# Taking out twenty waits between VectorE and GpSimd in a gated convolution and spectral-filter kernel

## The chip, the cores and the metric

The kernel runs on one core of one Trainium2 chip. The metric is the device time of one execution in microseconds (us). The engines are named as in the profile: PE (TensorE, matrix products into PSUM), DVE (VectorE), ACT (ScalarE), POOL (GpSimd, which works on SBUF alone and issues DMAs of its own), SP (SyncE, which here only issues DMAs).

## The reference, cut to what matters

Input q, k, v and x have 2048 positions and 640 channels. A first branch convolves k with a causal kernel of four taps per channel, multiplies by v, convolves the result with a causal kernel of 2048 taps per channel (by FFT) and multiplies by q. A second branch multiplies the two-dimensional spectrum of q by a complex weight. A gate, one number per position, mixes the two.

```python
def reference(A_q, A_k, A_v, A_shift_k, A_ssm_k, A_ssm_D, B_x, B_w_r, B_w_i, gate_w):
    x = A_q
    g = sigmoid((x * gate_w).sum(-1, keepdims=True))
    # a: k_shift = causal 4-tap convolution of k; kv = k_shift * v
    #    y = causal convolution of kv with ssm_k over 2048 positions + kv * ssm_D;  a = q * y
    # b: irfft2(rfft2(x) * (w_r + 1j * w_i))
    return g * a + (1 - g) * b
```

## The kernel before

All Fourier transforms are done as matrix products with constant matrices on PE, in stages of 32 and 64 points, with 32 by 32 block transposes on DVE between them. The work is cut into units, each with a name and a number, and each unit into operations numbered from 0:

- `fwd` u (u = 0 to 7): loads an eighth of q transposed (`xT`), folds it by four operations on SBUF, two adding and subtracting at L301 from XX into M, two at L303 from M back into XX, then multiplies on PE (L309, L316) and lets ACT copy the result into XX.
- `b1`, `bs2`, `i1`, `u`, `dic`: the second branch, the stages of the spectrum of q. In `bs2` the weight w multiplies the spectrum (L389, L392) and two operations at L395 combine the parts into XX. In `dic` ACT scales the result, two operations at L465 and two at L467 unfold it in M, and a DMA takes it to the output, added to what is there (POOL, L471) or plainly (SP, L474).
- `kv` u, `h` u (0 to 9): the first branch's data. `kv` loads k and v, makes the four-tap convolution on PE (L486), multiplies by v (DVE, L489), folds it in two operations at L495 and transposes (DVE, L498). `h` loads the long kernel, lets ACT negate one half (L507), adds another piece to it with an accumulating DMA that POOL issues (L508), and adds the ssm_D term in one short DVE operation (L511).
- `s1Y`, `s1H`, `s2`, `is1`, `afin`: transforms of kv and h on PE with DVE transposes into YY (L530, L540), their product in `s2` (PE L560, ACT L565, multiplications at L578 and L581, sums at L586), the inverse transform (PE L271, DVE L276), and in `afin` the product with q and the output.

The elementwise operations on SBUF are made by a helper `ttop` (L217). Each can run on POOL or on DVE; a set written out by hand, `ON_DVE` (L23), tells which run on DVE. The order in which everything is issued is written out as well, in `ORDER` (L40): each engine, and each of the two DMA queues that SP and POOL feed, works through its own part of that list in order. Semaphores between the engines follow from the tiles that operations read and write.

Every operation carries a pair `port` (L175, L220). The first number is 1 for what `ttop` made. The second is 1 where the operation, run on DVE, has both of its operands in SBUF; an operation of `ttop` that on DVE reads PSUM instead (those with `alt`, at L389, L578 and L628) has 0. `gate_cols` (L290) and the short operation of `h` (L512) are marked by hand. Beside the semaphores of the data, `_emit` (L702) adds a further wait when `GATE` (L34) is true: after each DVE operation marked with the second number, the next POOL operation in the list that is marked with the first waits for it, whether or not it has to do with its data. One wait stands for all DVE operations marked before it, and POOL operations behind it in the queue come later by themselves. DVE never waits for POOL on this ground.

Twenty pairs result. In the order of the list, unit number and operation number of POOL's operation behind those of DVE's:

| POOL waits at | for DVE's | POOL waits at | for DVE's |
|---|---|---|---|
| fwd 2 (4), L303 | fwd 2 (3), L303 | bs2 5 (4), L389 | bs2 0 (10), L395 |
| fwd 4 (2), L301 | kv 0 (5), L495 | bs2 3 (9), L395 | kv 6 (4), L495 |
| fwd 6 (2), L301 | fwd 6 (1), L301 | kv 9 (4), L495 | h 9, L511 |
| fwd 6 (4), L303 | kv 1 (5), L495 | s2 15 (11), L586 | s2 15 (10), L586 |
| fwd 7 (3), L303 | h 1, L511 | dic 1 (7), L465 | dic 1 (6), L465 |
| fwd 5 (2), L301 | fwd 5 (1), L301 | dic 4 (6), L465 | h 8, L511 |
| kv 4 (5), L495 | fwd 3 (4), L303 | kv 8 (4), L495 | dic 2 (7), L465 |
| kv 5 (4), L495 | h 3, L511 | dic 5 (8), L467 | dic 5 (7), L465 |
| s2 5 (4), L578 | s2 4 (10), L586 | dic 3 (9), L467 | dic 3 (8), L467 |
| s2 6 (10), L586 | h 4, L511 | dic 7 (9), L467 | dic 7 (8), L467 |

At dic 5 the operation waited for is also one whose result POOL's operation reads.

Of the kernel before, what the change touches and what calls it, by code (L numbers as in the profile page):

```python
# [30 lines left out]
    "afin": [(0, 4), (2, 4), (3, 4), (4, 4), (5, 4), (6, 4), (7, 4), (7, 6), (8, 4), (9, 4), (9, 6)],  # L31
    "dic": [(0, 9), (1, 6), (2, 6), (2, 7), (2, 8), (2, 9), (3, 7), (3, 8), (4, 8), (4, 9), (5, 6), (5, 7), (7, 6), (7, 7), (7, 8)],
}.items() for i, k in l}
GATE = True  # L34
HRAW = set()
FIRST=(3,3)
BACK={7,9}
# [664 lines left out]
def _emit(tc, plan):  # L702
# [4 lines left out]
    with tc.manual_schedule():  # L707
        for i in ORDER:
            o = plan.ops[i]
            made = o.fn()  # L710
            if GATE and o.eng == "DVE" and o.port[1]:
                ahead = made
# [70 lines left out]
```

## Time and profile before

| | us |
|---|---|
| three runs | 283.7, 286.7, 291.62 |
| their median | 286.7 |
| the profiled execution: time | 283.68 |
| its span, from first to last instruction | 281.6 |
| busy: PE, DVE, POOL, ACT | 246.3, 224.1, 150.1, 103.6 |

The profile is of one execution. Times in its rows count from the start of the span. In a row of the timeline stand the start, the length, the engine, the line of the kernel, the operation, what it writes and reads with the shapes, how many instructions the row holds, and in brackets the idle time of the engine before it and what ended that. In the chain of waits, each piece is what the next one waited for, up to the instruction that ended last; "issue" is time in which an engine waited for nothing that the profile can name, and a DMA counts from its issue to its landing. A transfer or an operation is named by the tile it writes and the tile it reads (XX<-xT). An operation that stands at its engine without getting its data shows as a longer one, not as idle time.

### The profile page before, as it was taken

Reading aid. Unit: us, or ns where it says so; the run is one execution under the profiler, and the core shown is the slowest. Engines: PE = TensorE matmul, PEld = TensorE weight load, DVE = VectorE, ACT = ScalarE, POOL = GpSimd, SP = SyncE. Lnnn points to the kernel's source line nnn. Section 1 sums busy time; section 2 is a strip of 40 time slices with the busy share of each in tenths; the row PEclk is TensorE's granted clock in tenths of the full one; section 3 lists DMA queues with packets and bytes.
Section 4 is the critical chain, followed back from the end, with each engine's and each line's share of the span. In section 5 each row is a group of like instructions: output and inputs, shape, how many; then the busy total and the mean of one; then the engine's idle time right before and its main releaser. Section 6 shows DMA issues by size and latency. Waiting matters only on the chain.

```text
span 281.6 us, 10200 instructions
## 1 busy us (share of the span) xinstructions
PE 246.3 (87%) x4562; PEld 144.9 (51%) x4562; DVE 224.1 (80%) x250; ACT 103.6 (37%) x232; POOL 150.1 (53%) x116
## 2 busy tenths in 40 slices
PE   0798789899999999788998988999999999999950
PEld 0674445554334454125445433667776677776450
DVE  3979489759998999999999999896464895664970
ACT  1052404451233333362263030546644374445500
POOL 0047557535005574798989710079888328339420
PEclk9999979999999999999999999999999999999996
DMA  7999979959996255687269963626548538737789
GB/s 277 421 416 346 330 264 420 410 123 365 278 389 230 70 98 199 188 338 254 82 165 352 260 121 99 276 80 231 146 115 139 131 54 149 228 54 97 134 200 211
DMA packets 28251, 61.53 MB, mean 218 GB/s; under 512 B 1712, under 2 KB 18480, under 8 KB 26544
## 3 DMA queue, kind: packets, MB, share of 16 engines
q1 hardware_dynamic: 22512, 51.45, 49.8%
q0 software_dynamic: 5696, 9.44, 21.9%
q8 instruction: 36, 0.59, 0.8%
q14 instruction: 7, 0.06, 0.1%
HBM read 50.39 MB, written 10.49 MB: 216 GB/s over the span
## 4 chain that ended last, share of the span: by engine, by line
PE 64%; DVE 15%; DMA 8%; POOL 5%; issue 4%; SPq 1%; ACT 1%; DVEq 0%; POOLq 0%; ACTq 0%
PE banks L560 11%; PE banks L271 11%; PE banks L356 7%; PE banks L447 7%; PE banks L420 7%; PE banks L530 5%; PE banks L622 5%; DMA XX<-xT 4%; DMA V<-h 4%; DVE YY L540 3%; DVE XX L276 3%; PE banks L309 3%; PE banks L453 2%; PE banks L486 2%; PE banks L428 2%
## 5 line engine op out<-in xcount | busy, mean ns | idle before, releaser
L540 DVE STREAM_TRANSPOSE YY<-banks 128x1024 f32<-128x1024 f32 x40 | 48.2, 1227 | 8.4 <-PE banks L530 8.4
L560 PE MATMUL banks<-YY,s2a 64*32 64x256 f32 x1280 | 43.0, 389 | 2.7 <-issue 1.6
L565 ACT ACTIVATE H<-banks 128x512 f32<-128x512 f32 x40 | 23.5, 598 | 39.9 <-PE banks L560 20.2
L495 POOL TENSOR_TENSOR T<-V 128x512 f32<-128x512 f32 x12 | 15.8, 1330 | 41.8 <-DVE V L489 22.0
L560 PEld LDWEIGHTS banks<-YY,s2a 64*32 64x32 f32 x1280 | 24.0, 105 | 19.7 <-issue 6.7
L271 PE MATMUL banks<-YY,ca 32*64 32x512 f32 x512 | 31.1, 607 | 0.6 <-DVE YY L540 0.4
L309 PE MATMUL banks<-cc,XX 128*64 128x162 f32 (+1 forms) x256 | 22.1, 330 | 8.7 <-DVE cc L287 8.7
L612 ACT ACTIVATE V<-V,g 128x128 f32<-128x128 f32 x72 | 21.9, 394 | 14.4 <-DMA V<-q 14.4
L309 PEld LDWEIGHTS banks<-cc,XX 128*64 128x64 f32 x256 | 19.4, 150 | 14.2 <-DVE cc L287 8.7
L581 DVE TENSOR_TENSOR YY<-banks,H 128x512 f32<-128x512 f32 x24 | 16.3, 682 | 13.1 <-ACT H L565 12.8
L276 DVE STREAM_TRANSPOSE YY<-banks 128x2048 f32<-128x2048 f32 x10 | 23.1, 2313 | 3.3 <-PE banks L271 2.9
L303 POOL TENSOR_TENSOR XX<-M 128x640 f32<-128x640 f32 x8 | 12.4, 1557 | 19.3 <-DVE XX L303 13.7
L461 ACT ACTIVATE M<-banks,om 128x320 f32<-128x320 f32 x32 | 14.2, 528 | 21.9 <-PE banks L453 16.2
L395 POOL TENSOR_TENSOR XX<-M,M 128x642 f32<-128x642 f32 x15 | 19.7, 1328 | 4.1 <-DVE M L389 3.4
L271 PEld LDWEIGHTS banks<-YY,ca 32*64 32x64 f32 x512 | 13.3, 129 | 15.5 <-issue 10.6
L356 PE MATMUL banks<-XX,cb 128*128 128x512 f32 (+1 forms) x42 | 20.9, 632 | 0.0
L622 PEld LDWEIGHTS banks<-YY,is2a 128*64 128x64 f32 x320 | 18.1, 134 | 5.3 <-DVE YY L540 1.9
L622 PE MATMUL banks<-YY,is2a 128*64 128x128 f32 x320 | 20.3, 279 | 0.5 <-DVE YY L276 0.5
L447 PEld LDWEIGHTS banks<-di,L 128*128 128x128 f32 x128 | 17.6, 190 | 5.5 <-ACT L L436 3.0
L586 POOL TENSOR_TENSOR YY<-M,M 128x512 f32<-128x512 f32 x14 | 18.5, 1355 | 3.4 <-DVE M L578 1.1
L420 PE MATMUL banks<-cc,XX 128*128 128x128 f32 x128 | 19.4, 295 | 0.4 <-DVE M L578 0.4
L447 PE MATMUL banks<-di,L 128*128 128x160 f32 x128 | 19.5, 306 | 0.0
(70 smaller groups left out, 417.3 us busy)
## 6 DMA issues: line engine op xcount, KB each, us to landing
G<-k SPq DMA_DIRECT2D x10, 1024.0 KB, 8.3
L<-w SPq DMA_DIRECT2D x8, 642.0 KB, 4.7
XX<-xT SPq DMA_DIRECT2D x8, 640.0 KB, 8.7
V<-v SPq DMA_DIRECT2D x10, 512.0 KB, 6.7
V<-h SPq DMA_DIRECT2D x10, 512.0 KB, 9.0
V<-h POOLq DMA_DIRECT2D x10, 512.0 KB, 8.0
V<-q SPq DMA_DIRECT2D x10, 512.0 KB, 5.6
out_dram<-V SPq DMA_DIRECT2D x8, 512.0 KB, 4.6
```

What stands on the lines that cost most here:

```text
L271: mm(p[h * 64:h * 64 + 64, j, :nd * 8], is1[r, sg, ri, :], v[r, h * 2 + src, :, d0:d0 + nd, :].rearrange("p m d e -> p d m e"), start=(i = ...
L276: nc.vector.transpose(by_col(x, d0, nd), p[:, :, :nd * 8].rearrange("p j (d i) -> p d j i", i=8))
L309: mm(bk(p, g_)[ri * 64:ri * 64 + 64, o:o + n], X[:, s, g_ * 64:g_ * 64 + 64], df[:, 0, ri * 323 + o:ri * 323 + o + n], start=(o == 0), sto ...
L356: mm(v(x)[:, e0:e0 + ne], m1b, by_col(XX, d0 + a + e0, ne), start=True, stop=True)
L395: ttop(642, lambda f, ri=ri, o=o, dst=dst: f(dst(), T(t1)[:, ri], T(t2)[:, 1 - ri], op=o), us=1.28, r=[t1, t2, ("t", i, 0, ri), ("t", i, 1 ...
L420: mm(psa[:, t, :, b, :], row(XX, n2)[:, t * 161:t * 161 + 128], W(n2), start=True, stop=True)
L447: mm(bk(p, b)[:, n * 160:n * 160 + 160], U[:, t_, r_], di[:, b * 160:b * 160 + 160], start=(n == 0), stop=False)
L540: op("DVE", dve(1024), lambda b=b: nc.vector.transpose(by_col(YY[:, :, y], a * 64 + b * 32, 32), view(b)), r=[p[b]], w=yk)
L560: mm(ps(p)[j * 32:j * 32 + 32, h].rearrange("p (y r d) -> p y r d", y=2, r=2)[:, :, ri], s2a[r, k, ri * 32:ri * 32 + 32], YY[r, k // 2, y0 ...
L565: op("ACT", act_us(512), lambda p=p, hs=hs: act(sb(hs, 2, 256), ps(p)[:, :, 256:], AF.Copy), r=[p], w=[hs])
L612: act(dst(j), src(j), AF.Copy, scale=g[:, n0 + j:n0 + j + 1])
L622: mm(v()[b * 64:b * 64 + 64, j, :], is2a[:, n2, :], row(YY[:, :, yp], n2), start=True, stop=True)
```

## The change

`GATE` is set to false, so `_emit` adds none of the twenty waits. The order on every engine, the engine of every operation, the slots of all tiles, the DMAs and the waits for data are as before.

```diff
@@ -31,7 +31,7 @@
     "afin": [(0, 4), (2, 4), (3, 4), (4, 4), (5, 4), (6, 4), (7, 4), (7, 6), (8, 4), (9, 4), (9, 6)],
     "dic": [(0, 9), (1, 6), (2, 6), (2, 7), (2, 8), (2, 9), (3, 7), (3, 8), (4, 8), (4, 9), (5, 6), (5, 7), (7, 6), (7, 7), (7, 8)],
 }.items() for i, k in l}
-GATE = True
+GATE = False
 HRAW = set()
 FIRST=(3,3)
 BACK={7,9}
```

The code that it switches off:

```python
            if GATE and o.eng == "DVE" and o.port[1]:
                ahead = made
            elif ahead is not None and o.eng == "POOL" and o.port[0]:
                tc.add_manual_dep(made.ins, ahead.ins.name, ...)
                ahead = None
```

## The prediction

> **What bounds the kernel now.** I read the page first (busy shares, then the chain by engine), then the chain of waits in order of time, then the timelines of POOL and VectorE at each of the 20 places.
>
> ```profile
> span 281.6 us, 10200 instructions
> PE 246.3 (87%) x4562; PEld 144.9 (51%) x4562; DVE 224.1 (80%) x250; ACT 103.6 (37%) x232; POOL 150.1 (53%) x116
> PE 64%; DVE 15%; DMA 8%; POOL 5%; issue 4%; SPq 1%; ACT 1%; DVEq 0%; POOLq 0%; ACTq 0%
> ```
>
> TensorE is busy for 87% and carries 64% of the chain; VectorE has 15%, POOL only 5%. So an earlier POOL is worth something only in the few places where the chain passes through it, while a later VectorE is worth three times as much. The chain in order of time (start, length, what):
>
> ```profile
> 5.04 10.88 DMA XX<-xT
> 15.96 2.60 issue
> 18.60 1.57 POOL M L301
> ...
> 22.58 1.55 POOL M L301
> 24.20 1.50 POOL XX L303
> 25.70 10.43 DMA V<-h
> 36.15 0.22 DVE V L511
> ...
> 36.47 1.49 PE banks L530 x32
> ...
> 106.17 1.19 DVE XX L361
> ...
> 116.67 0.82 DVE XX L395
> ```
>
> The reader is to see the 2.60 us of "issue" at 15.96: the data of POOL's L301 (unit fwd 4) had landed at 15.92, yet it starts at 18.60. That is one of the 20 waits, on the chain. The same chain then runs through POOL's L301 of fwd 6 (also one of the 20), L303, the accumulating DMA of h that POOL issues at 25.70, and TensorE's L530 at 36.47. Later pieces of the chain are VectorE's own (106.17, 116.67), beside two more of the 20 places.
>
> **What the two engines do to each other.** The waits keep POOL from starting while an earlier VectorE operation with both operands in SBUF is unfinished; the other order, VectorE starting while POOL works, they leave free, and the trace has it twice. POOL and VectorE timelines (start, length, line, operation, count, idle time before it), then the durations of the two lines (least, median, most):
>
> ```profile
> 41.25 1.28 POOL L495 TENSOR_TENSOR T<-V 128x512 f32<-128x512 f32 x1 [1.69 <-DVE V L489]
> 42.25 0.83 DVE L495 TENSOR_TENSOR T<-V 128x512 f32<-128x512 f32 x1
> 210.68 3.20 POOL L467 TENSOR_TENSOR M<-M 128x640 f32<-128x640 f32 x2
> 211.57 0.75 DVE L511 TENSOR_TENSOR V<-V,gd 128x32 f32<-128x32 f32 x1
> L495 DVE TENSOR_TENSOR T<-V x8: 679/685/828, 16.5 to 228.5; 128x512 f32<-128x512 f32 x8
> L511 DVE TENSOR_TENSOR V<-V,gd x10: 170/175/751, 32.4 to 211.6; 128x32 f32<-128x32 f32 x10
> ```
>
> L495 at 42.25 took 0.83 where its line's median is 0.685, and ends at 43.08, 0.55 after POOL's L495 ended (41.25 + 1.28 = 42.53). L511 at 211.57 took 0.75 where the median is 0.175; POOL's first L467 ended at about 210.68 + 1.60 = 212.28, and L511 ends at 212.32. So a VectorE operation with two SBUF operands that meets a running POOL operation stands until that one ends, and then needs 0.55 us (512 elements) or next to nothing (32). That is the price of this change: at each place POOL's gain is at most its wait, and VectorE's loss is up to one POOL operation, 1.3 to 1.6 us.
>
> **The change, place by place.** Nothing is computed, moved or issued otherwise; 20 waits go, and the semaphore wait itself costs nothing that a row shows. What is late next is in each case POOL's other input or VectorE.
>
> ```profile
> 16.48 0.69 DVE L495 TENSOR_TENSOR T<-V 128x512 f32<-128x512 f32 x1
> 18.55 1.25 DVE L498 STREAM_TRANSPOSE T<-T 128x1024 f32<-128x1024 f32 x1
> 20.19 1.56 DVE L303 TENSOR_TENSOR XX<-M 128x640 f32<-128x640 f32 x2 [0.40 <-POOL M L301]
> 20.84 1.04 POOL L508 DMA_DIRECT2D V<-h  x1 [0.69 <-ACT V L507]
> 21.67 0.82 DVE L301 TENSOR_TENSOR M<-XX 128x640 f32<-128x640 f32 x1
> 32.35 0.17 DVE L511 TENSOR_TENSOR V<-V,gd 128x32 f32<-128x32 f32 x1
> 32.97 1.22 PE L530 MATMUL banks<-V,ca 32*32 32x512 f32 x32
> 36.47 1.49 PE L530 MATMUL banks<-V,ca 32*32 32x512 f32 x32 [2.27 <-DVE V L511]
> 36.51 3.06 POOL L303 TENSOR_TENSOR XX<-M 128x640 f32<-128x640 f32 x2 [4.41 <-DVE V L511]
> ```
>
> *fwd 4 and fwd 6 (the chain's 2.60).* POOL's L301 starts at 15.97 and ends at 17.54. VectorE's L495 at 16.48 now stands until 17.54 and ends at 17.54 + 0.55 = 18.09 instead of 17.17, 0.92 late; behind it L301, L495 and L498 are late by as much. The L303 pair at 20.19 had waited 0.40 for POOL's L301, which is now long done, so it is late by 0.92 - 0.40 = 0.5. POOL's queue meanwhile stops at the h DMA, which waits for ScalarE until 20.84 as before and ends at 21.88. There POOL's second L301 (fwd 6) would be free 0.70 sooner than 22.58, but VectorE's L303 and L301 stand end to end until 22.49 + 0.5 = 23.0. Which of the two a waiting port goes to, no row shows; I take VectorE, because its next operation begins before the last one is done (the x2 rows: 1.56 for two of 0.82), so POOL starts at about 23.1. L303 needs both L301, the DMA of h is issued at 26.2 and lands 0.5 late: +0.5 on the chain. Bounds: -0.7 if POOL's operations hold nothing up, +2.1 if POOL goes between (0.5 and one more operation of 1.6).
>
> *fwd 7.* The longest gap, 4.41 us before 36.51, goes: POOL's L303 starts when its queue is free, at 32.1 (36.51 - 4.41). L511 at 32.35 stands behind it, up to 1.3 us, and TensorE's L530 at 32.97 with it. That is hidden by the 2.27 us that TensorE then waits for the second h before 36.47; without that cover it would cost 1.3. Nobody gets anything for the earlier L303: its reader comes behind that L530 in TensorE's order. Zero.
>
> TensorE's clock falls in this stretch (windows: busy time of each engine, granted clock, DMA share, GB/s):
>
> ```profile
> 34.20:36.46 2.26, 0.00 (x0) 0.02 (x1) 0.31 (x2) 0.62 (x2) 0.00 (x0) 1.00 1.03 401
> 37.34:40.75 3.41, 3.41 (x40) 1.10 (x26) 3.24 (x4) 0.00 (x0) 2.23 (x2) 0.50 0.48 197
> ```
>
> After 2.26 us without a matmul the clock is at half for 3.41 us, which costs at most 1.7 us of TensorE's work. Here the gap gets shorter, 2.27 - 1.3 + 0.5 = 1.5 us, and whether that still drops the clock no row shows: between 0 and -1.7, I take 0, as the only gap in this stretch that is shown did drop it. [...]
>
> ```profile
> 103.98 1.27 POOL L578 TENSOR_TENSOR M<-M,H 128x512 f32<-128x512 f32 x1
> 105.60 0.29 DVE L511 TENSOR_TENSOR V<-V,gd 128x32 f32<-128x32 f32 x2
> 106.06 2.55 POOL L586 TENSOR_TENSOR YY<-M,M 128x512 f32<-128x512 f32 x2 [0.80 <-DVE V L511]
> 106.17 1.25 DVE L361 STREAM_TRANSPOSE XX<-banks 128x1024 f32<-128x1024 f32 x1 [0.28 <-PE banks L356]
> 117.62 4.25 POOL L389 TENSOR_TENSOR M<-M,L 128x642 f32<-128x642 f32 x3 [1.97 <-DVE XX L395]
> 248.16 0.69 DVE L581 TENSOR_TENSOR YY<-banks,H 128x512 f32<-128x512 f32 x1 [4.36 <-ACT H L565]
> ```
>
> *s2 6 at 106.* POOL's L586 starts at 105.3, when L578 is done, and runs 1.27. The L511 pair at 105.60 stands until 106.57 and ends near 106.77 instead of 105.89, 0.88 late; L361 behind it had waited 0.28, so VectorE is 0.6 late where the chain is VectorE's: +0.6. POOL's own 0.8 is not on the chain. Bounds: 0, and +1.9 if POOL's second L586 goes between the two L511.
>
> *bs2 5 at 117.* POOL's L389 starts at 115.65 instead of 117.62 and lasts 4.25 / 3 = 1.4; VectorE's L395 at 116.67 (in the chain) stands until 117.05: +0.4. The next L389 waits for a ScalarE copy, so POOL gains nothing. Bounds 0 and +1.4.
>
> *The others.* At dic 3 VectorE's L467 loses about 1 us, which the 4.36 us before 248.16 hide (without them it costs the 1.0). At the rest POOL's operation either waits for something else as long, or comes free while VectorE's operation is running or about to. I take such a one as standing until VectorE is done, as with the wait: zero. Bounds: 0 to the 1.3 to 1.6 of one POOL operation, should POOL be let in first. [...]
>
> **Sum.** 0.5 + 0.6 + 0.4 = +1.5 us. The profiled execution took 283.68 (span 281.6 and 2.1 around it), which gives 285.2. The three runs shown are 283.7, 286.7 and 291.62, so this execution is the lowest of them and 3.0 below the median. A median of a few such runs I place halfway, 1.5 above the profiled one: 286.7. All cases below are on that footing (own sum + 1.5).
>
> **The rivals.**
> - *The gain comes through.* If VectorE isn't held up, the chain gets 0.7 at fwd 6: 283.68 - 0.7 + 1.5 = 284.5. With the whole 2.60 it would be 282.6. For it: the 2.60 is on the chain. Against: L495 and L511 stretched exactly to POOL's end, and POOL's queue stands at 20.84 for ScalarE in any case.
> - *The clock stays up* at 37: 286.7 - 1.7 = 285.0. For it: a gap of 1.5 instead of 2.27. [...]
> - *It does nothing.* If the port puts POOL behind VectorE in the same places, the time is 283.68 + 1.5 = 285.2. Against: at 15.97, 32.1, 105.3 and 115.65 VectorE isn't in such an operation when POOL comes free.
> - *Slower: POOL is let in between.* Place: where VectorE operations with two SBUF operands stand end to end and POOL waits beside them (fwd 2, fwd 6 twice, fwd 5, the second L511 at 105.6, kv 8, dic 7: seven places). Price: one POOL operation each, 1.3 to 1.6. It decides from about three of them on the path (1.5 + 3 x 1.5 = 6.0); with four it is 286.7 + 6.0 = 292.7. Against: at 211.57 VectorE got in between POOL's two L467, not the reverse; the tail of several is hidden by waits for TensorE.
>
> **Chances.** The sum of small losses 0.50, nothing happens 0.15, the gain comes through 0.12, the clock stays up 0.13, POOL in between 0.10. About 2% (5.7 us) is what a measurement of this kernel can tell from no change: 281.0 to 292.4. Faster than that needs the whole 2.60 and the clock together, or a gain later that I don't see: 0.05. Slower needs four or more places: 0.10. Same: 0.85. The range, 281.5 to 291.5, reaches to the whole 2.60 at the low end and to three places at the high end; the likeliest case alone is 284 to 290, by the bounds of its terms.
>
> **What would show it.** POOL's L301 of fwd 4 near 16.0 and a VectorE L495 beside it stretched to some 1.6 us; the issue of the second h no earlier than before; an L511 near 105.6 of about 1 us; L395 near 117 of about 1.1; VectorE's busy time up by 3 to 6 us at the same count. The prediction is wrong if those rows keep their medians while POOL overlaps them, if POOL's operations themselves get longer by more than VectorE's 0.8, or if TensorE shows new idle time between 180 and 260, where I count on it to hide VectorE's losses.

## The result and the profile after

| | before | after |
|---|---|---|
| median (six runs each) | 284.75 us | 297.77 us |
| ratio | | 1.038, 95% interval 1.0276 to 1.0484 |
| span of the profiled execution | 281.6 us | 295.1 us |

Some executions of either kernel are slower than the rest at a lower clock (after: 298.68 to 299.69 us at a mean granted clock of 0.959 to 0.964, the rest at 0.968 and 0.969; before, in later runs: 288.99 and 289.05 us at 0.975, the rest at 0.981 to 0.991), so the ratios here and below leave them out: on average 295.3 us against 284.5, which is 3.8% or 10.8 us (13.0 between the medians of all six, 13.5 between the profiled spans). The profile of the changed kernel, in the lines that were shown of before, and the row of the clock that TensorE was granted in 40 slices (tenths):

```profile
span 295.1 us, 10196 instructions
PE 250.2 (85%) x4562; PEld 145.6 (49%) x4562; DVE 238.5 (81%) x250; ACT 103.6 (35%) x232; POOL 153.0 (52%) x116
PE 59%; DVE 29%; issue 4%; DMA 4%; POOL 1%; ACT 1%; DVEq 0%; ACTq 0%
PEclk9998779999999999999999899999999999999996
```

The same 250 VectorE instructions take 14.4 us more, and VectorE's share of the chain goes from 15% to 29%. POOL's falls from 5% to 1%. TensorE takes 3.9 us more for the same matmuls, in the slices with a 7 and an 8. The longest pieces of VectorE's in the new chain:

```profile
28.39 5.91 DVE T L495 x2
...
159.52 4.85 DVE T L495
```

They are the two L495 of kv 1 at 28.39 and the one of kv 6 at 159.52. Timelines of VectorE and POOL at the two places (start, length, line, operation, count):

```profile
28.39 5.90 DVE L495 TENSOR_TENSOR T<-V 128x512 f32<-128x512 f32 x2
26.36 0.88 POOL L508 DMA_DIRECT2D V<-h  x1
26.97 1.84 POOL L303 TENSOR_TENSOR XX<-M 128x640 f32<-128x640 f32 x1
28.49 3.30 POOL L301 TENSOR_TENSOR M<-XX 128x640 f32<-128x640 f32 x2
31.86 3.83 POOL L303 TENSOR_TENSOR XX<-M 128x640 f32<-128x640 f32 x2
...
159.52 4.85 DVE L495 TENSOR_TENSOR T<-V 128x512 f32<-128x512 f32 x1
156.33 1.32 POOL L578 TENSOR_TENSOR YY<-YY,H 128x512 f32<-128x512 f32 x1
157.61 1.57 POOL L389 TENSOR_TENSOR M<-M,L 128x642 f32<-128x642 f32 x1
159.11 0.86 POOL L508 DMA_DIRECT2D V<-h  x1
159.72 2.89 POOL L395 TENSOR_TENSOR XX<-M,M 128x642 f32<-128x642 f32 x2
162.29 1.52 POOL L495 TENSOR_TENSOR T<-V 128x512 f32<-128x512 f32 x1
```

At 159.52 VectorE stands until 164.37, and POOL's last operation there ends at 162.29 + 1.52 = 163.81: the 0.55 us that an operation of 512 elements needs, counted from the end not of one POOL operation but of three. By the records all three began after VectorE's, the first of them 0.20 us after it (159.72). At 28.39 the first L495 of the pair stands 3.95 us in the same way, for the rest of an L303 that was running and for two L301; the second stands 2.03, for one more L303. The reader is to see two more things. In front of both groups stands a DMA that POOL issues (L508). And behind it POOL's records overlap: the pair of L395 ends at 162.61, POOL's L495 begins 0.32 before that. Ahead of the DMA the overlap is 0.04 (156.33 + 1.32 = 157.65 against 157.61).

The gap that opens behind each costs a second time. TensorE's timeline, then the windows in which its clock is down (length, busy time of PE, PEld, DVE, ACT and POOL, granted clock, DMA share, GB/s):

```profile
25.94 1.11 PE L486 MATMUL banks<-G,gd 64*32 64x512 f32 x16 [3.23 <-DVE YY L540]
35.63 2.02 PE L530 MATMUL banks<-T,ca 32*32 32x512 f32 x32 [3.89 <-DVE T L498]
167.37 5.26 PE L271 MATMUL banks<-YY,ca 32*64 32x512 f32 x64 [3.83 <-DVE M L389]
26.89:30.30 3.41, 3.41 (x34) 2.93 (x28) 3.25 (x3) 0.00 (x0) 3.41 (x4) 0.50 1.06 308
33.72:40.54 6.82, 4.91 (x54) 2.91 (x56) 4.42 (x6) 0.00 (x0) 1.97 (x2) 0.50 0.77 317
166.84:170.25 3.41, 2.88 (x32) 1.14 (x40) 3.41 (x3) 1.46 (x5) 3.29 (x3) 0.50 0.41 167
```

TensorE waits 3.89 us before 35.63 and 3.83 before 167.37, and its clock is at half from within each gap on, for 6.82 and 3.41 us. A third gap, of 3.23 us before 25.94 (1.12 in before), belongs to neither place: it grew at fwd 6, where VectorE's two L303 take 3.38 us instead of 1.56 (shown further down), and it too is followed by 3.41 us at half clock.

### The profile page after: what moved, and what is told of

Read it like the earlier page. It is cut to its first block, busy times and chain, and to the rows that moved or that the text cites. A ratio compares the mean times of both kernels' runs of the same rounds, so it can differ in the third digit from the quotient of the medians.

```text
span 295.1 us, 10196 instructions
## 1 busy us (share of the span) xinstructions
PE 250.2 (85%) x4562; PEld 145.6 (49%) x4562; DVE 238.5 (81%) x250; ACT 103.6 (35%) x232; POOL 153.0 (52%) x116
## 4 chain that ended last, share of the span: by engine, by line
PE 59%; DVE 29%; issue 4%; DMA 4%; POOL 1%; ACT 1%; DVEq 0%; ACTq 0%
PE banks L271 10%; PE banks L560 10%; PE banks L420 6%; PE banks L447 6%; PE banks L356 6%; PE banks L530 5%; DVE YY L540 5%; DVE T L495 5%; PE banks L309 4%; PE banks L622 4%; DVE XX L276 3%; DMA V<-out_dram 2%; DVE YY L276 2%; PE banks L486 2%; DVE V L489 2%
## 5 line engine op out<-in xcount | busy, mean ns | idle before, releaser
L495 POOL TENSOR_TENSOR T<-V 128x512 f32<-128x512 f32 x12 | 16.6, 1391 | 57.0 <-DVE V L489 57.0
L560 PE MATMUL banks<-YY,s2a 64*32 64x256 f32 x1280 | 42.4, 389 | 3.6 <-DVE YY L578 1.2
L271 PE MATMUL banks<-YY,ca 32*64 32x512 f32 x512 | 32.7, 631 | 4.5 <-DVE M L389 3.8
L309 PE MATMUL banks<-cc,XX 128*64 128x162 f32 (+1 forms) x256 | 24.7, 356 | 8.6 <-DVE cc L287 8.6
L309 PEld LDWEIGHTS banks<-cc,XX 128*64 128x64 f32 x256 | 21.3, 165 | 14.7 <-DVE cc L287 8.6
L395 POOL TENSOR_TENSOR XX<-M,M 128x642 f32<-128x642 f32 x15 | 20.0, 1366 | 7.9 <-DVE M L389 7.6
L271 PEld LDWEIGHTS banks<-YY,ca 32*64 32x64 f32 x512 | 12.6, 135 | 21.6 <-issue 12.7
L303 POOL TENSOR_TENSOR XX<-M 128x640 f32<-128x640 f32 x8 | 14.0, 1763 | 15.3 <-DVE M L301 15.2
L436 ACT ACTIVATE L<-banks 128x640 f32<-128x640 f32 x16 | 11.3, 709 | 27.0 <-PE banks L428 27.0
```

Source lines behind the costliest of these rows:

```text
L271: mm(p[h * 64:h * 64 + 64, j, :nd * 8], is1[r, sg, ri, :], v[r, h * 2 + src, :, d0:d0 + nd, :].rearrange("p m d e -> p d m e"), start=(i = ...
L309: mm(bk(p, g_)[ri * 64:ri * 64 + 64, o:o + n], X[:, s, g_ * 64:g_ * 64 + 64], df[:, 0, ri * 323 + o:ri * 323 + o + n], start=(o == 0), sto ...
L495: ttop(512, lambda f, s=s, o=o: f(sb(f_, 2, 16, 32)[:, s], sb(v_, 16, 2, 32)[:, :, 0], sb(v_, 16, 2, 32)[:, :, 1], op=o), r=[v_], w=[f_])
L560: mm(ps(p)[j * 32:j * 32 + 32, h].rearrange("p (y r d) -> p y r d", y=2, r=2)[:, :, ri], s2a[r, k, ri * 32:ri * 32 + 32], YY[r, k // 2, y0 ...
```

## The experiments

The two places were read off the trace; whether they carry the loss, and whether the DMA issue or the full queue behind it makes POOL pass VectorE, had to be tried. Theory A: the loss is mostly these two places. A1: a DMA issue is what lets POOL's next operations pass; the expectations call POOL "out of step" then, after the overlap of its records (0.32 us here), and the parts of POOL that they speak of are a guess of the author's that no run shows. A2: any operations that stand ready in POOL's queue pass. A3: the issue or its transfer keeps a hold for some time. Theory B: many places of one POOL operation each add up.

**Two waits back, or only those two out.** The waits are chosen by POOL's operation.

```diff
 GATE = True
+WAITS = [('bs2', 3, 9), ('fwd', 6, 4)]
...
+                if o.key in WAITS:
                     tc.add_manual_dep(made.ins, ahead.ins.name, ...)
```

> 18 of the 20 waits are out, two stand: fwd 6 (4) behind kv 1, and bs2 3 (9) behind kv 6. In the changed kernel VectorE's L495 stood there for 3.95 and 4.85 us, across three POOL operations each. Theory A (the loss is mostly these two places, where several POOL operations pass a standing VectorE operation): about 9 of the 13 us come back, some 286 to 289 us for a median where before has 284.8 and the changed kernel 297.8; both L495 near their 0.69. Theory B (many places with one POOL operation each add up): at most 4 us come back, 293 to 295.

287.94 us, ratio 1.0114 (1.0051 to 1.0177) to the runs of before beside it. Theory A holds: with 2 of the 20 waits, 2.7 of the 3.8% are gone. The other eighteen together are worth 1.1%.

The reverse keeps eighteen (`if o.key not in NO_WAIT`, with the same two keys).

> The reverse: only those two waits are out, 18 stand. Theory A: 8 to 10 us slower than before, L495 of kv 1 and of kv 6 at 3 to 5 us. Theory B: at most 4 us slower.

293.77 us, ratio 1.033 (1.0217 to 1.0443). So 3.3% for the two and 1.1% for the eighteen stand beside 3.8% for all, within their intervals. One more execution of the same kernel shows the two places.

> The same kernel as eighteen_waits, for a profile at full clock: L495 of kv 1 and of kv 6 each stand until POOL's queue runs dry, 3 to 5 us; VectorE is late by 3 to 4 us behind the first and by 4 more behind the second, and TensorE's clock is at half for one or two stretches of 3.4 us.

That execution took 289.96 us, less than the 291.67 to 296.03 of the four behind the ratio, and the timelines of VectorE and POOL show one reason:

```profile
26.24 2.39 DVE L496 TENSOR_TENSOR T<-V 128x512 f32<-128x512 f32 x2
28.75 3.07 POOL L302 TENSOR_TENSOR M<-XX 128x640 f32<-128x640 f32 x2 [1.28 <-DMA XX<-xT]
...
L496 DVE TENSOR_TENSOR T<-V x8: 678/688/4844, 15.7 to 234.5; 128x512 f32<-128x512 f32 x8
```

At kv 6 the operation stands for 4.84 again, but the pair of kv 1 takes only 2.39: here POOL's next operation waited for a load that landed after POOL came to it, and in that pause of 1.28 us VectorE got in. The expectation was met at one place and not at the other; what the place at kv 1 costs hangs on when a load lands.

**The DMA issues moved.** Without any waits, and with the two issues elsewhere in POOL's queue.

```diff
-GATE = True
+GATE = False
-    ... 229, 230, 244, 250, 37, 231, 77, 78, 39, 41, 234, 235, 251, 38, ...
+    ... 229, 230, 244, 250, 251, 37, 231, 77, 78, 39, 41, 234, 235, 38, ...
-    ... 172, 661, 171, 163, 173, 164, 637, 494, ...
+    ... 172, 171, 163, 173, 164, 637, 661, 494, ...
```

> No waits, and two of POOL's DMA issues moved in its queue: h 1 to directly behind ScalarE's negation (ahead of fwd 6), h 7 to behind the three operations bs2 3 (9), bs2 3 (10), kv 6 (5). In the changed kernel both long rows lie right behind such an issue, and the POOL operations there overlap by 0.3 us in the records. Theory A1 (a DMA issue puts POOL's parts out of step, and then no moment comes at which VectorE gets in): L495 of kv 1 and of kv 6 stand for one POOL operation at most, under 2.2 us each, and the time falls to 287 to 291. Theory A2 (operations that stand ready in POOL's queue pass VectorE, DMA or not): L495 of kv 6 still stands for about 4 us, time above 293.

288.79 us, ratio 1.0149 (1.007 to 1.0227), and the longest L495 takes 2.03 (1.61 at kv 6). That is A1 and not A2. But moving h 1 also changes when it lands, so the place at kv 6 was then tried by itself: one wait out, and the same with h 7 behind the three operations.

```diff
 GATE = True
+NO_WAIT = [('bs2', 3, 9)]
...
+                if o.key not in NO_WAIT:
                     tc.add_manual_dep(made.ins, ahead.ins.name, ...)
```

> One wait is out, that of bs2 3 (9), which stands behind POOL's DMA issue of h 7 and ahead of three POOL operations that need nothing of each other. Theory A1 (out of step behind an issue): VectorE's L495 of kv 6 stands for 4.8 us, some 4 us later VectorE, and TensorE's clock at half behind the gap: 4 to 7 us slower than before. If one place cannot cost that much, under 2 us.

> The same wait out, and the DMA issue of h 7 behind the three operations instead of ahead of them. Theory A1: POOL is in step, L495 of kv 6 stands for the rest of one POOL operation, 0.7 to 2 us, and the time is within 2 us of before. If POOL's full queue is the cause and not the issue, it stands for 4 us as in the run beside it.

One wait out costs 2.5% (1.0189 to 1.0311), 291.05 against 284.4 us. With the issue behind the three operations it costs 0.3% (1.0001 to 1.0058), 285.11. VectorE, POOL and TensorE in the first and then in the second:

```profile
153.83 4.83 DVE L496 TENSOR_TENSOR T<-V 128x512 f32<-128x512 f32 x1
153.41 0.85 POOL L509 DMA_DIRECT2D V<-h  x1
154.02 2.87 POOL L396 TENSOR_TENSOR XX<-M,M 128x642 f32<-128x642 f32 x2
156.58 1.51 POOL L496 TENSOR_TENSOR T<-V 128x512 f32<-128x512 f32 x1
161.64 5.33 PE L272 MATMUL banks<-YY,ca 32*64 32x512 f32 x64 [3.74 <-DVE M L390]
```

```profile
153.05 1.61 DVE L496 TENSOR_TENSOR T<-V 128x512 f32<-128x512 f32 x1
152.78 3.07 POOL L396 TENSOR_TENSOR XX<-M,M 128x642 f32<-128x642 f32 x2
155.81 1.27 POOL L496 TENSOR_TENSOR T<-V 128x512 f32<-128x512 f32 x1
157.01 0.87 POOL L509 DMA_DIRECT2D V<-h  x1
157.65 3.84 PE L272 MATMUL banks<-YY,ca 32*64 32x512 f32 x64 [0.53 <-DVE M L390]
```

The same three POOL operations stand ready in both. In the second VectorE waits for the rest of the first of them alone, 1.61, and gets in between the two L396. TensorE's gap shrinks from 3.74 to 0.53, and its 64 matmuls take 3.84 instead of 5.33: in the first the clock is at half from 161.24 to 164.65, in the second it is full there. So 3.2 us of VectorE's, and 1.5 of TensorE's at half clock behind them, are 4.7 of the 5.9 us between the two medians.

**The price by itself.** Small cases between barriers, three times each; POOL's and VectorE's operations are of 128x512, VectorE's first ones read PSUM and only set when its operation with two SBUF operands arrives. All of the kernel's own work is left out. A case gives, in this order, how many VectorE operations read PSUM, how many behind them have two SBUF operands, how many operations POOL has, whether each of these reads the one before it, and whether POOL issues a DMA ahead of them.

```python
CASES = [..., (1, 1, 4, 0, 0), (3, 1, 4, 0, 1), (3, 1, 8, 0, 1), ..., (1, 4, 4, 0, 0), ...]
...
for first, two, pool, chained, dma in CASES:
    ...
    if dma:
        nc.gpsimd.dma_start(Z, I["h"][rep][:, :1024], accum_op=OP.add)
    for i in range(pool):
        src = PO[i - 1] if chained and i else B
        nc.gpsimd.tensor_tensor(PO[i], src, A, op=OP.add)
    for i in range(first):
        nc.vector.tensor_tensor(DO[i], banks[:, 0], B, op=OP.mult)
    for i in range(two):
        nc.vector.tensor_tensor(DO[first + i], B, C, op=OP.add)
```

> The kernel's work is left out: eleven small cases, three times each, between barriers. POOL runs 4 or 8 operations on SBUF of 128x512 (1.27 us each in the kernel), VectorE arrives during the first with one operation of two SBUF operands (0.69 alone). Theory A1: with independent POOL operations and no DMA ahead VectorE's takes 1 to 1.8 us; with a DMA issue ahead of 4 operations it takes 4 to 5 us and of 8 operations 9 to 10; where each POOL operation reads the one before, 1 to 1.8 us with and without the DMA. Theory A2: 4 to 5 us with 4 and 9 to 10 with 8 independent operations, DMA or not. VectorE operations that read PSUM keep 0.68 in all. Where VectorE has four operations end to end and POOL one, POOL gets in after the first or second by what the changed kernel showed, behind all four by what the prediction took.

Four cases, POOL's row and then VectorE's: four operations; the same behind a DMA issue; eight behind an issue; four against four of VectorE's.

```profile
98.57 5.37 POOL L45 TENSOR_TENSOR PO<-B,A 128x512 f32<-128x512 f32 x4 [0.86 <-ACT B L40]
99.07 1.31 DVE L49 TENSOR_TENSOR DO<-B,C 128x512 f32<-128x512 f32 x1
...
105.56 5.20 POOL L45 TENSOR_TENSOR PO<-B,A 128x512 f32<-128x512 f32 x4
106.50 4.83 DVE L49 TENSOR_TENSOR DO<-B,C 128x512 f32<-128x512 f32 x1
...
113.03 10.05 POOL L45 TENSOR_TENSOR PO<-B,A 128x512 f32<-128x512 f32 x8
113.97 9.68 DVE L49 TENSOR_TENSOR DO<-B,C 128x512 f32<-128x512 f32 x1
...
149.65 6.26 POOL L45 TENSOR_TENSOR PO<-B,A 128x512 f32<-128x512 f32 x4 [0.80 <-ACT B L40]
150.22 6.25 DVE L49 TENSOR_TENSOR DO<-B,C 128x512 f32<-128x512 f32 x4
```

Without an issue VectorE's operation takes 1.31 and is through before POOL's second operation is; behind an issue it takes 4.83 and 9.68, to the end of POOL's queue however long that is. Where both have four ready, they take turns, and each loses the time of the other: VectorE's four take 6.25 where three alone, in the second probe, take 1.88. Of the cases that are not shown, eight operations without an issue let VectorE in after 1.31, operations that read one another after 1.31 and, behind an issue, after 1.19; and one POOL operation against four of VectorE's got in after the first of them (its row takes 1.70 us, one alone 1.26). All three repetitions agree within 0.2 us. Whether A1 or A3 holds, the second probe tells, in which POOL has to wait for something after the issue.

```python
CASES = [("IIIII", "PPPPT"), ("DIIII", "PPPPPPP"), ("DIIII", "PPPTT"), ("DICIII", "PPPPPPPT"), ("DAIII", "PPPPPT"), ("D", "PTTT"),
         ("IIDII", "PT"), ("IIDIII", "PPPPPPT")]
```

The first string is POOL's queue: D an issue, I an independent operation, C one that reads the one before, A one that waits for ScalarE. The second is VectorE's: P reads PSUM, T has two SBUF operands.

> The kernel's work is left out: eight small cases, three times each, between barriers. In the first probe a VectorE operation with two SBUF operands stood for 4.83 and 9.68 us behind a POOL DMA issue and 4 or 8 independent operations, and 1.31 without the issue. Theory A1 (after the issue POOL's parts are out of step, until an operation waits for something): behind issue, operation, one that reads it, three independent ones, VectorE arriving in the third operation stands for 1.3; behind issue, an operation that waits for ScalarE, three independent ones, also 1.3; an issue in the middle of the queue (two operations, issue, three operations) makes it stand to the end of the queue if it arrives behind the issue, and 1.3 if it arrives in the first operation. Rival A3 (the issue keeps a hold on the ports as long as its transfer runs, or for some us): it stands to the end of the queue in the two cases with a wait as well. Both: five operations without issue 1.3; VectorE operations that read PSUM keep 0.68; an issue with no POOL operation behind it delays VectorE by nothing.

Three cases: issue, an operation, one that reads its result, three independent ones; issue, an operation that waits for ScalarE, three independent ones; two operations, issue, three operations.

```profile
99.26 0.88 POOL L45 DMA_DIRECT2D Z<-h  x1 [2.26 <-ACT B L39]
102.73 4.15 POOL L47 TENSOR_TENSOR PO<-B,A 128x512 f32<-128x512 f32 x3
103.19 1.36 DVE L52 TENSOR_TENSOR DO<-B,C 128x512 f32<-128x512 f32 x1
...
107.91 0.88 POOL L45 DMA_DIRECT2D Z<-h  x1 [1.02 <-ACT B L39]
110.41 1.25 POOL L47 TENSOR_TENSOR PO<-L,A 128x512 f32<-128x512 f32 x1 [1.62 <-ACT L L42]
110.64 1.57 DVE L52 TENSOR_TENSOR DO<-B,C 128x512 f32<-128x512 f32 x1
...
133.91 0.87 POOL L45 DMA_DIRECT2D Z<-h  x1
134.51 3.98 POOL L47 TENSOR_TENSOR PO<-B,A 128x512 f32<-128x512 f32 x3
134.96 4.08 DVE L52 TENSOR_TENSOR DO<-B,C 128x512 f32<-128x512 f32 x1
```

After a wait of POOL's, for its own result or for another engine, VectorE gets in after one operation (1.36, 1.57), though the issue lies only 3.9 and 2.7 us back; behind an issue in the middle of a queue it stands to the end (4.08). A3 falls. The moment at which VectorE arrives doesn't decide it either: behind an issue it stood having come 0.45 and 0.94 us into a POOL operation, and without one it got in having come 0.50 and 1.07 us into it. VectorE operations that read PSUM aren't held behind an issue (seven took 4.27 us, 0.61 each), and an issue with nothing behind it delays nothing (the three that took 1.88). What an issue changes in POOL, no row shows. What the traces of before and after have is the overlap of POOL's records by 0.31 to 0.34 us, three times in before (at 98.80, 196.83 and 198.05) and seven times in after, each time in a row behind an issue. Whether anything other than a DMA issue does the same, no run tried.

**The prediction's first step by itself.** One wait out, that of fwd 4 (2).

```diff
+NO_WAIT = [('fwd', 4, 2)]
```

> One wait alone is out, that of fwd 4 (2), the 2.60 us on the chain of before. By the prediction's first step: VectorE's L495 near 16.5 stretched to 1.7, VectorE 0.5 late behind it, and the whole 0.5 us slower. If the gain comes through, 0.7 to 2.6 faster.

0.9993 (0.9969 to 1.0016), 284.53 us: no difference, and none of the 2.60 comes through. L495 near 16.4 took 1.85, and the operations behind it came 0.56 us later than in before; that delay doesn't show in the whole time either.

**A faster version.** The waits stay, and the issues move, both in the first kernel and h 1 alone (the first pair of lines) in the second.

```diff
-    ... 244, 250, 37, 231, 77, 78, 39, 41, 234, 235, 251, 38, ...
+    ... 244, 250, 251, 37, 231, 77, 78, 39, 41, 234, 235, 38, ...
-    ... 172, 661, 171, 163, 173, 164, 637, 494, ...
+    ... 172, 171, 163, 173, 164, 637, 661, 494, ...
```

> All 20 waits stand, and the two DMA issues are moved as in the run without waits. On the chain of before lies the landing of h 1, 10.4 us behind its issue at 25.7, and TensorE stands 2.3 us for it and then has half its clock for 3.4 us. If the landing follows the issue, h 1 lands some 2 us sooner and the time falls by 2 to 4 us, to 281 to 283 where before has 285. If the transfers in front of it set the landing, the time stays within 1 us of before.

> All 20 waits stand, and only the DMA issue of h 1 is moved ahead of fwd 6. With both issues moved the time was 0.5% under before, h 1 landed 2.5 us sooner and TensorE's clock stayed up. If h 1 alone does it, 283 where before has 284.5.

With both moved the time is 283.12 us, ratio 0.9953 (0.9921 to 0.9985): the one version under both kernels, by half a per cent. h 1 lands 2.5 us sooner and the clock stays at full from 12 to 275 us in its profile (mean granted clock 0.991, in that of before 0.984). With h 1 alone the ratio is 0.9992 (0.9955 to 1.0029). There h 1 lands 2.4 us sooner, and in the profile the clock is down at another place, for 3.41 us from 73.6 (mean 0.983). The two intervals overlap. So it isn't shown that the earlier landing gives the half per cent; whether it does, or moving h 7, or the chance of how many gaps bring the clock down, stays open.

## Why the prediction was wrong

The forecast was 286.7 us and no measurable change, from a loss of 1.5 us; it was 297.8, and the loss 10.8 us by the runs compared. That it could become slower was left to a rival that got 0.10.

- *VectorE stands behind a running POOL operation, and then needs 0.55.* Right. At fwd 4 POOL started at 15.97 as forecast and VectorE's L495 took 1.73; at s2 6 the pair of L511 took 1.18 where 105.60 to 106.77 was forecast; at bs2 5 L395 took 0.96, for 1.1 forecast. As delays of VectorE the terms +0.5 and +0.6 were about right, and +0.4 was some 0.14. As times they are not shown: with only the wait of fwd 4 out VectorE came 0.56 later and the whole took the same (0.9993).
- *Who is next when both stand ready.* Wrong. The prediction let VectorE go on, since its operations begin before the last is done. At fwd 6 POOL got in between the two L303, by which VectorE came some 2.2 us later instead of 0.5 (the +2.1 that was the bound there); and in the probe the two take turns:

```profile
20.61 3.38 DVE L303 TENSOR_TENSOR XX<-M 128x640 f32<-128x640 f32 x2
21.44 1.86 POOL L301 TENSOR_TENSOR M<-XX 128x640 f32<-128x640 f32 x1
```

At fwd 6 POOL's operation stands behind an issue too (L508 at 20.68), so that place is no clean case of taking turns. At fwd 5 it is one: POOL's L301 at 49.29 has no issue ahead of it and gets in between VectorE's L495 and L301, which takes 2.18. These two and kv 8 are among the eighteen waits that cost 1.1% together.
- *"The others ... zero. Bounds: 0 to the 1.3 to 1.6 of one POOL operation."* This is the step that failed. kv 1 and kv 6 were among the others. POOL's operation was taken to stand until VectorE is done, and the bound was one POOL operation. At kv 6 POOL went first though its operation began 0.20 us after VectorE's, and the price at both places was up to three operations: 3.95 and 4.85 us for an L495 of 0.69. Behind a DMA issue every operation that stood ready in the queue went first: three at kv 6, and in the probe VectorE stood for 9.68 us, to the end of eight. In the trace of before L508 stood in front of both places, as here at kv 6:

```profile
152.23 0.68 DVE L495 TENSOR_TENSOR T<-V 128x512 f32<-128x512 f32 x1
151.81 0.82 POOL L508 DMA_DIRECT2D V<-h  x1
153.10 2.60 POOL L395 TENSOR_TENSOR XX<-M,M 128x642 f32<-128x642 f32 x2 [0.47 <-DVE T L495]
```

The 0.47 us is the whole wait; taken out by itself it cost 2.5%. What wasn't in that trace was a VectorE operation with two SBUF operands that arrived among POOL operations behind an issue: the two from which the price was read met POOL where its records don't overlap (at 41.25 it had waited 1.69 us for VectorE, and at 210.68 it began 0.07 us after its L465 ended). A bound taken from them held only for their state.
- *The clock.* The prediction weighed one gap of 2.27 us and took no change. The change made three gaps of 3.23, 3.89 and 3.83 us, and with each the clock went to half, for 3.41, 6.82 and 3.41 us. How long a gap has to be for that, the rows don't settle: the clock fell 0.95 us after the end of the gap of 3.23 (from 25.94 to 26.89), 2.0 us into the one of 3.89 (which begins at 31.74) and 3.3 into the one of 3.83, and in before 0.87 us after the end of one of 2.27 (from 36.47 to 37.34).
- *The slower rival.* POOL let in between, at one operation a place, 292.7 with four. The direction was right, and one of the two places was on its list (the second of fwd 6 is the wait for kv 1), but at the price of one operation. The place that carries most, kv 6 with 2.5% alone, it didn't list.

## What to carry to other kernels

A wait that orders two engines may look idle and still hold back something far dearer than the time it takes: ask what stands ready in the other engine's queue, not only what it does next. Where POOL issues a DMA and has independent work on SBUF behind it, keep VectorE operations with two SBUF operands away from there (in the probe one took 4.83 us behind an issue and four operations, 1.31 without the issue), put the issue behind that work, or let POOL wait once after it (in the probe one wait was enough, for its own result, 1.36, or for another engine, 1.57). A price read off the trace holds for the state in which it was read; before it is used as a bound, look for the states (behind a DMA issue, behind a wait) that no row of it covers.

## What the runs showed of the hardware that was not expected

- Behind a DMA that POOL issues, independent POOL operations kept VectorE's operations with two SBUF operands out to the end of the queue: 4.83 us with four operations, 9.68 with eight, against 1.31 without the issue. One wait of POOL's ended that (1.36 and 1.57).
- With no issue ahead, the two engines took turns operation by operation, also where VectorE's own operations follow each other without a gap: four against four took 6.25 us, which is 1.56 for each of VectorE's instead of 0.68.
- TensorE's clock went to half with gaps between matmuls of 2.27 us (before) and 3.23 us (after), and 2.0 us into one of 3.89 (after).
